# Attention and a bilinear GLU on one core: q, k and v made in five groups of columns instead of six

## The chip, the core and the metric

The kernel runs on one core of one Trainium2 chip. The time is that of one execution on the device, in microseconds (us). The engines are named as in the profile: PE is the matrix engine (PEld its weight load), DVE the vector engine, ACT the scalar engine, POOL the general one, SP the engine that mostly issues transfers (DMAs). A page of the profile describes one execution; the times are medians of several.

## What is computed

x has 2048 rows of 640. It is normalised by row (no gain or bias); the result goes into an attention with a sliding, dilated window and into a feed-forward product of two gates without a nonlinearity between them.

```python
xn = _layernorm(x)
qkv = (xn @ wqkv).reshape(B, S, 3, H, Dh)          # H = 32 heads of Dh = 20
off = jnp.arange(8) * 2                            # window 8, dilation 2
logits = einsum("bhsd,bhswd->bhsw", q, k[pos - off]) * Dh ** -0.5   # masked where pos < off
s = einsum("bhsw,bhswd->bhsd", softmax(logits), v[pos - off]).reshape(B, S, D) @ wo
g = _silu(((xn @ w_gate) * (xn @ w_up)) @ w_down)  # inner width F = 1536
out = x + s * g
```

## The kernel before

**Arithmetic.** Every product is made of three matmuls on operands of type fp32r: each operand is split into a high part (a copy by ACT) and a low part (what is left, a subtraction by POOL or DVE), and high·high, high·low and low·high are added up in PSUM (`ALL3`). `split` (L104, L105) makes the two parts; a split of weights is thus one instruction on ACT and one on POOL behind it.

**q, k and v.** The 32 heads are cut into column groups, `GROUPS = [5, 5, 5, 5, 6, 6]`; the tokens are cut in two halves r = 0, 1. A unit u is a group and a half, twelve in all. `qkv(u, i)` makes one of the eight token tiles of a unit: 15 matmuls (three parts times five blocks of the inner dimension) of 128 × 128 by 3 × heads × 20 columns, so 300 or 360, into one PSUM bank. Below, these 15 are called a product. ACT copies the bank into a staging buffer (L409; three buffers, each for two products), and after each second product a DMA on ACT's queue (L411) writes it to a scratch array in memory. The banks go round in the order `q_one`, g, u; g and u have two banks each, so the bank of `q_one` comes round at every third product.

**The weights of a group.** `load_wq` (L129) loads the raw weights of group g+1 with two DMAs on SP when the second product of group g begins; `split_wq` (L143) splits its five blocks one after the other in the first five products of the group's second half (L105 with 128 × 300 or 128 × 360). High and low parts of blocks 0 to 3 lie in two rotating slots out of ten, those of block 4 in a slot that is kept.

**What runs beside.** `attention` (L424) is a generator that yields the cost of each piece; `advance(budget)` runs pieces as long as there is credit, so many microseconds after each product, 0.38 a head. For each unit it copies q to PSUM (ACT, L469), and in four rounds multiplies q by the shifted k (DVE, L478), reduces (DVE, L488), multiplies the weights of the unit before by its v (DVE, L452) and adds those up (POOL, L455); then comes the softmax (exp on ACT, L511). `load_kq` and `load_kv` (L379 to L387, SP) fetch q, k and v of the next unit from the scratch array, `zero_kv` (L360, POOL) clears the rows before the first token when the width of a unit changes, `store_o` (L530, SP) writes the result. `ORDER` is the order of the units.

`differences` (L1086) is a second row of work: sums and differences of 128 × 512 pieces of x that the groups of gate and up products need later. They are cut into steps, and after each product `paced` grows by 0.42 (0.8 in the last two units); each whole number runs one step. A step is one addition on POOL (L1097, L1099, L1105, L1107, L1109), or a copy on ACT (L1092) with a subtraction on POOL behind it (L1093).

**The order.** It is written out by hand: each engine takes its instructions in the order in which the program writes them. The loop at L1282 runs over units 2 to 11:

```python
            if g + 1 < len(GROUPS) and (r, i) == (0, 1):
                load_wq(g + 1, ((0, 3), (3, 5)))
            elif g + 1 < len(GROUPS) and r and i < KD:
                split_wq(g + 1, nc.gpsimd, (i, i + 1))
```

**Around it.** Ahead of the loop lie the start (normalisation, transposes, units 0 and 1 and the first two blocks of gate and up, L114). Behind it, `group(f)` for f = 2 to 11 (L1179, matmuls L1214) makes gate and up products with fewer multiplications out of the differences and of sums of weights (`w_add` L1164, `w_split`), with plain products (L114) between; `advance` goes on there. In the group before the last, `begin_last` runs what is left of the attention and loads wo (L611). Then come the output product (L950) and the down products (L813).

## Time and profile before

| | |
|---|---|
| median of three runs | 756.78 us (755.92 to 756.83) |
| the profiled execution | 757.46 us, of which the span from the first to the last instruction 755.5 us |
| granted clock of PE | 0.999 of full |
| PE between 60 and 310 us | busy without a break |
| idle time of PE | 9.0 us, nearly all in the first 60 us and behind 540 us |
| stages by the profile | start to 101 us, loop over units 2 to 11 to 277, groups to 540, output and down products to the end |

In the profile a row of grouped instructions reads: line, engine, operation, output and input by the program's names, shape, count, then busy time, mean ns of one, and the idle time of the engine in front of them with what ended it. A chain is followed back from the last instruction; each of its rows has a start, a length and what ran.

### The profile page before, as it was taken

The page shows a single profiled execution, that of the slowest core. Times are in us where ns is not written, and L with a number is a line of the kernel's source. Part 1 is how long each engine was busy: PE and PEld are TensorE (multiplying, and loading weights), DVE is VectorE, ACT ScalarE, POOL GpSimd, SP SyncE. Part 2 cuts the span into 40 slices and gives each one's busy share as a digit, 9 for nine tenths or more (in the row PEclk, how much of TensorE's full clock was granted, in tenths as well). Part 3 has the DMA queues.
Part 4 walks back from the last instruction along what each step waited for, and adds up shares of the span by engine and source line. Part 5 has one row for each costly group of instructions (what it writes and reads, how often), then busy time and mean ns, then how long its engine had stood idle before and what let it go on. Part 6 is the DMA issues. An engine that isn't in the chain of part 4 may idle for free.

```text
span 755.5 us, 11592 instructions
## 1 busy us (share of the span) xinstructions
PE 746.5 (99%) x4342; PEld 687.7 (91%) x4342; DVE 599.2 (79%) x753; ACT 278.5 (37%) x534; POOL 421.5 (56%) x342
## 2 busy tenths in 40 slices
PE   8999999999999999999999999999999999999997
PEld 6889899999999998888888888888999999999997
DVE  7899996998887977979697977335898697777775
ACT  4334213233333333232322222234465664444442
POOL 5100247788968969799879796855659800000000
PEclk9999999999999999999999999999999999999999
DMA  8463446586566473655355222543577565555534
GB/s 316 156 192 102 127 140 188 187 240 180 163 198 196 128 209 95 162 157 174 97 140 165 77 65 66 173 114 105 167 192 211 188 254 188 189 189 188 188 105 140
DMA packets 101974, 123.01 MB, mean 163 GB/s; under 512 B 24376, under 2 KB 75956, under 8 KB 101918
## 3 DMA queue, kind: packets, MB, share of 16 engines
q1 hardware_dynamic: 84318, 107.77, 46.7%
q10 hardware_dynamic: 17600, 14.50, 6.0%
q8 instruction: 34, 0.56, 0.3%
q14 instruction: 22, 0.18, 0.1%
HBM read 78.73 MB, written 42.81 MB: 161 GB/s over the span
## 4 chain that ended last, share of the span: by engine, by line
PE 92%; DVE 3%; POOL 2%; issue 1%; DMA 1%; ACT 0%; SPq 0%; DVEq 0%; POOLq 0%
PE u L114 12%; PE g L114 12%; PE q L400 10%; PE g L400 8%; PE u L400 8%; PE q L813 7%; PE g L1214 7%; PE u L813 6%; PE u L1214 5%; PE e L813 4%; PE g L813 3%; PE q L114 2%; PE q L1214 2%; PE q L950 2%; PE u L950 1%; PE e L950 1%
## 5 line engine op out<-in xcount | busy, mean ns | idle before, releaser
L455 POOL TENSOR_TENSOR o<-o,t 128x800 f32<-128x800 f32 (+1 forms) x81 | 164.3, 2029 | 60.8 <-DVE o L452 50.8
L105 POOL TENSOR_TENSOR s<-wraw,s 128x768 fp32r<-128x768 f32 (+5 forms) x72 | 89.0, 1252 | 77.6 <-ACT s L104 71.4
L478 DVE TENSOR_TENSOR t<-q,kv 128x1600 f32<-128x1600 f32 (+1 forms) x48 | 92.5, 1928 | 11.9 <-ACT q L469 6.1
L114 PE MATMUL g<-xc,s 128*128 128x512 f32 (+1 forms) x435 | 100.4, 382 | 0.0
L114 PE MATMUL u<-xc,s 128*128 128x512 f32 (+1 forms) x435 | 100.4, 382 | 0.0
L114 PEld LDWEIGHTS u<-xc,s 128*128 128x128 f32 x435 | 79.7, 188 | 15.7
L114 PEld LDWEIGHTS g<-xc,s 128*128 128x128 f32 x435 | 79.5, 188 | 15.7 <-DVE gh L1202 0.2
L488 DVE TENSOR_REDUCE lg<-t 128x80 f32<-128x1600 f32 (+1 forms) x48 | 92.3, 1924 | 0.1
L452 DVE TENSOR_TENSOR t<-e,kv 128x800 f32<-128x800 f32 (+1 forms) x84 | 87.2, 1038 | 5.3 <-POOL o L455 5.2
L400 PE MATMUL q<-s,xc 128*128 128x300 f32 (+1 forms) x540 | 84.6, 307 | 1.2 <-DVE lg L252 0.6
L400 PEld LDWEIGHTS q<-s,xc 128*128 128x128 f32 x540 | 79.4, 188 | 2.5 <-DVE lg L252 0.8
L104 ACT ACTIVATE s<-wraw 128x640 fp32r<-128x640 f32 (+5 forms) x73 | 43.0, 603 | 62.0 <-PE u L114 35.8
L400 PE MATMUL g<-s,xc 128*128 128x300 f32 (+1 forms) x420 | 65.8, 308 | 0.0
L400 PE MATMUL u<-s,xc 128*128 128x300 f32 (+1 forms) x420 | 65.4, 307 | 0.0
L400 PEld LDWEIGHTS g<-s,xc 128*128 128x128 f32 x420 | 62.4, 188 | 0.0
L400 PEld LDWEIGHTS u<-s,xc 128*128 128x128 f32 x420 | 62.1, 188 | 0.0
L813 PE MATMUL q<-xc,s 128*128 128x320 f32 x285 | 46.3, 309 | 0.0
L813 PEld LDWEIGHTS q<-xc,s 128*128 128x128 f32 x285 | 42.9, 188 | 0.0
L1214 PE MATMUL g<-xc,s 128*128 128x512 f32 x150 | 37.3, 389 | 0.0
L1186 ACT ACTIVATE gh<-g 128x512 f32<-128x512 f32 x30 | 17.9, 598 | 50.7 <-PE g L1214 50.7
L776 DVE TENSOR_TENSOR s<-s,s 128x768 fp32r<-128x768 f32 x29 | 27.8, 958 | 8.9 <-ACT s L772 8.8
L1214 PEld LDWEIGHTS g<-xc,s 128*128 128x128 f32 x150 | 28.1, 188 | 5.8
(328 smaller groups left out, 1331.5 us busy)
## 6 DMA issues: line engine op xcount, KB each, us to landing
h_scr<-gh SPq DMA_DIRECT2D x48, 256.0 KB, 2.7
wraw<-in_wgu SPq DMA_DIRECT2D x11, 640.0 KB, 4.1
t<-h_scr SPq DMA_DIRECT2D x8, 768.0 KB, 7.5
kv<-qkv_scr SPq DMA_DIRECT2D x14, 400.0 KB, 5.1
qkv_scr<-s ACTq DMA_DIRECT2D x18, 300.0 KB, 4.2
s_scr<-gh SPq DMA_DIRECT2D x16, 320.0 KB, 3.7
gh<-s_scr SPq DMA_DIRECT2D x16, 320.0 KB, 3.8
gh<-in_x SPq DMA_DIRECT2D x16, 320.0 KB, 4.4
```

Of the source, the lines that this page charges most:

```text
L104: nc.scalar.activation(hi, raw, AF.Copy)
L105: eng.tensor_sub(lo, raw, hi.bitcast(F32))
L114: nc.tensor.matmul(acc, a, b, start=first and n == 0, stop=last and n == len(runs) - 1)
L400: nc.tensor.matmul(p, xT[(r * NE + i) // TPC][a][:, k, t0:t0 + P], wq[g][b][k], start=n == 0, stop=n == len(runs) - 1, skip_group_check=ac ...
L452: nc.vector.tensor_mul(t.rearrange("p (n d) -> p n d", d=DH), e[:, :, w].unsqueeze(2).to_broadcast([P, NE * nh, DH]), v)
L455: return NE * c * cost, lambda: eng.tensor_add(y, y, t)
L478: nc.vector.tensor_mul(t, q, k)
L488: nc.vector.tensor_reduce(out=lg[:, :, j:j + 2].rearrange("p n a -> p a n"), in_=t.rearrange("p a (n d) -> p a n d", d=DH), op=ALU.add, ax ...
L776: nc.vector.tensor_sub(hT[m][:, 1], h_raw[n][name], hT[m][:, 0].bitcast(F32))
L813: nc.tensor.matmul(p, y[:, i, k], wd_t[name][k][:, l], start=new and r == 0, stop=r == len(runs) - 1, skip_group_check=True)
L950: nc.tensor.matmul(b, y, w, start=new and r == 0, stop=r == len(runs) - 1, skip_group_check=True)
L1214: nc.tensor.matmul(y, w, x, start=j in (0, 1, 5) and r == 0, stop=r == len(runs) - 1, skip_group_check=True)
```

## The change

The column groups of the attention become `[6, 6, 4, 4, 6, 6]`, and a new table says which of them are made together: `MADE = [[0], [1], [2, 3], [4], [5]]`. The products now go over m, the entries of this table: 360 columns each, but 480 in the third, which makes q, k and v of two groups of four heads at once. There are 80 products (16 each) where there were 96. Calls of `qkv` in the start pass `(0, r, i)` in place of the unit. The two units that a broad product makes have one staging buffer (`wide`, two of them) and go out with two DMAs.

The weights of the broad group take four slots of three blocks of 512 columns; its raw weights come in three DMAs, the last (block 4) written behind the split of block 1. In every group the load of the next weights is written ahead of the first product, and the five blocks are split ahead of the products 3, 4, 6, 8 and 10 of sixteen, counted from 0 over both halves. The steps of `differences` go by a table of rates, one for each m and half. Their results are put into slots by k first.

```diff
@@ -29,9 +29,11 @@
 NCH = S // CH
 TPC = CH // P
 HALF = D // 2
-GROUPS = [5, 5, 5, 5, 6, 6]
+GROUPS = [6, 6, 4, 4, 6, 6]
+MADE = [[0], [1], [2, 3], [4], [5]]
 GOFF = [sum(GROUPS[:g]) * DH for g in range(len(GROUPS))]
 CMAX = max(GROUPS) * DH
+MC = [sum(GROUPS[g] for g in m) * DH for m in MADE]
 QB = 32
 NQ = P // QB
 QC = D // NQ
@@ -128,8 +130,8 @@
 
     def load_wq(g, parts, ahead={}):
 
-        c3 = 3 * GROUPS[g] * DH
-        wq_raw[g] = []
+        c3 = 3 * MC[g]
+        wq_raw.setdefault(g, [])
         for p in parts:
             t = st([P, p[-1] - p[0], c3], "wraw", 2)
             for k0, k1 in zip(p, p[1:]):
@@ -141,10 +143,14 @@
     fifth = []
 
     def split_wq(g, eng, ks=(0, KD)):
-        c3 = 3 * GROUPS[g] * DH
+        c3 = 3 * MC[g]
         if not fifth:
             fifth.append(slot([P, 4, 3 * 128]))
-        if g not in wq:
+        if g not in wq and MC[g] > CMAX:
+            y = [slot([P, 3, CH])[:, :, :c3] for _ in range(4)]
+            wq[g] = [[y[n // 3][:, n % 3] for n in range(a * KD, a * KD + KD)] for a in range(2)]
+            wq[g].append(None)
+        elif g not in wq:
             cols = -(-c3 // 64) * 64
             hi, lo = (slot([P, KD - 1, cols])[:, :, :c3] for _ in range(2))
             wq[g] = [[y[:, k] for k in range(KD - 1)] + [fifth[0][:, g % 2 * 2 + a, :c3]] for a, y in enumerate((hi, lo))]
@@ -153,7 +159,10 @@
             for a, b in ((k0, min(k1, KD - 1)), (max(k0, KD - 1), k1)):
                 a, b = max(a, ks[0]), min(b, ks[1])
                 if a < b:
-                    hi, lo = (y[:, a:b] for y in wq[g][2]) if a < KD - 1 else (y[KD - 1].unsqueeze(1) for y in wq[g][:2])
+                    if b - a > 1:
+                        hi, lo = (y[:, a:b] for y in wq[g][2])
+                    else:
+                        hi, lo = (y[a].unsqueeze(1) for y in wq[g][:2])
                     split(eng, t[:, a - k0:b - k0], hi, lo)
 
     wf_raw, wf = {}, {}
@@ -343,7 +352,8 @@
 
 
     UN = [(g, r) for g in range(len(GROUPS)) for r in range(DIL)]
-    ORDER = [0, 1, 2, 3, 4, 5, 6, 8, 7, 10, 9, 11]
+    ORDER = [0, 1, 2, 3, 4, 6, 5, 7, 8, 10, 9, 11]
+    wide, now = [], [None]
     q_t, kv_t, kv_buf, kv_zero, scr, staged, made = {}, {}, {}, {}, {}, [], set()
 
     def view_kv(u, b):
@@ -360,16 +370,16 @@
             nc.gpsimd.memset(kv_t[u][0:1, a, 0:W - 1, :], 0.0)
             kv_zero[b, a] = GROUPS[UN[u][0]]
 
-    def begin_unit(u):
-        g, r = UN[u]
-        c = GROUPS[g] * DH
-        if u:
-            scr[u] = dr.tile([P, 3, NE, c], F32, name=f"qkv_scr_{u}")
-            return
-        q_t[u] = st([P, NE, c], "q", 1)
-        view_kv(u, r)
-        for a in range(2):
-            zero_kv(u, r, a)
+    def begin_unit(m, r):
+        for g in MADE[m]:
+            u, c = 2 * g + r, GROUPS[g] * DH
+            if u:
+                scr[u] = dr.tile([P, 3, NE, c], F32, name=f"qkv_scr_{u}")
+            else:
+                q_t[u] = st([P, NE, c], "q", 1)
+                view_kv(u, r)
+                for a in range(2):
+                    zero_kv(u, r, a)
 
     def load_kq(u):
@@ -388,30 +398,38 @@
 
     ALL_RUNS = [(a, b, k) for a, b in ALL3 for k in range(KD)]
 
-    def qkv(u, i, runs=ALL_RUNS, at=None, act=None):
-
-        g, r = UN[u]
-        c = GROUPS[g] * DH
+    def qkv(m, r, i, runs=ALL_RUNS, at=None, act=None):
+
+        c = MC[m]
         p = pt([P, 3 * c], "q", 3)
         t0 = (i % TPC) * P
         for n, (a, b, k) in enumerate(runs):
             if n == at:
                 act()
-            nc.tensor.matmul(p, xT[(r * NE + i) // TPC][a][:, k, t0:t0 + P], wq[g][b][k], start=n == 0,
+            nc.tensor.matmul(p, xT[(r * NE + i) // TPC][a][:, k, t0:t0 + P], wq[m][b][k], start=n == 0,
                              stop=n == len(runs) - 1, skip_group_check=act is not None)
-        if u:
+        if m or r:
             if not staged:
                 y = slot([P, 2, 2 * 3 * CMAX], F32)
                 staged.extend([y[:, 0], y[:, 1], st([P, 2 * 3 * CMAX], "pk", 1)])
+            if c > CMAX and not wide:
+                wide.extend([slot([P, 6 * c], F32), st([P, 6 * c], "pk", 1)])
             if i % 2 == 0:
-                staged.insert(0, staged.pop())
-            y = staged[0][:, :6 * c].rearrange("p (a i c) -> p a i c", a=3, c=c)
-            nc.scalar.activation(y[:, :, i % 2, :], p.rearrange("p (a c) -> p a c", a=3), AF.Copy)
-            if i % 2:
-                nc.scalar.dma_start(scr[u][:, :, i - 1:i + 1, :], y)
-            if i == NE - 1:
-                made.add(u)
+                now[0] = wide if c > CMAX else staged
+                now[0].insert(0, now[0].pop())
+            n = len(MADE[m])
+            y = now[0][0][:, :6 * c].rearrange("p (n a i c) -> p n a i c", n=n, a=3, i=2)
+            nc.scalar.activation(y[:, :, :, i % 2, :].rearrange("p n a c -> p a n c"),
+                                 p.rearrange("p (a n c) -> p a n c", a=3, n=n), AF.Copy)
+            for k, g in enumerate(MADE[m]):
+                if i % 2:
+                    nc.scalar.dma_start(scr[2 * g + r][:, :, i - 1:i + 1, :], y[:, k])
+                if i == NE - 1:
+                    made.add(2 * g + r)
+            if c > CMAX and (r, i) == (DIL - 1, NE - 1):
+                staged.clear()
             return
+        u = 0
         nc.scalar.activation(kv_t[u][:, :, W - 1 + i, :], p[:, c:].rearrange("p (a c) -> p a c", a=2), AF.Copy)
         nc.scalar.activation(q_t[u][:, i, :], p[:, :c], AF.Copy)
         for i0, i1 in ((1, 5), (5, NE)):
...
@@ -1070,7 +1088,7 @@
     f0, f1 = KF - 2, KF - 1
     tt, tw, steps = [], {}, []
     T_UNIT = {(j, a, k): divmod(n, 3) for n, (j, a, k) in
-              enumerate((j, a, k) for j in ("T1", "T2", "T3") for a in range(2) for k in range(2))}
+              enumerate((j, a, k) for k in range(2) for j in ("T1", "T2", "T3") for a in range(2))}
 
     def t_unit(j, a, k):
@@ -1279,27 +1297,32 @@
 
     steps += [differences(k) for k in range(2)]
     paced = 0.0
-    for u in range(2, len(UN)):
-        begin_unit(u)
-        g, r = UN[u]
+    last, BLOCK = len(MADE) - 1, (3, 4, 6, 8, 10)
+    RATE = ((1.0, 0.4), (0.3, 0.2), (0.4, 0.6), (0.8, 0.8))
+    for m, r in ((m, r) for m in range(1, len(MADE)) for r in range(DIL)):
+        begin_unit(m, r)
+        heads, broad = MC[m] // DH, m < last and MC[m + 1] > CMAX
         for i in range(NE):
-            if g + 1 < len(GROUPS) and (r, i) == (0, 1):
-                load_wq(g + 1, ((0, 3), (3, 5)))
-            elif g + 1 < len(GROUPS) and r and i < KD:
-                split_wq(g + 1, nc.gpsimd, (i, i + 1))
-            if u == len(UN) - 3 and i == 6:
+            n = r * NE + i
+            if m < last and n == 0:
+                load_wq(m + 1, ((0, 2), (2, 4)) if broad else ((0, 3), (3, 5)))
+            elif m < last and n in BLOCK:
+                split_wq(m + 1, nc.gpsimd, (BLOCK.index(n), BLOCK.index(n) + 1))
+            elif broad and n == BLOCK[1] + 1:
+                load_wq(m + 1, ((4, 5),))
+            if (m, r, i) == (last - 1, 1, 6):
                 load_wf(2)
-            qkv(u, i)
+            qkv(m, r, i)
             if i == 1:
                 finish_piece()
-            advance(PACE * GROUPS[g] * 0.38)
-            paced += 0.42 if u < len(UN) - 2 else 0.8
+            advance(PACE * heads * 0.38)
+            paced += RATE[m - 1][r]
             while paced >= 1:
                 paced -= 1
                 step()
-        if u == len(UN) - 3:
+        if (m, r) == (last - 1, 1):
             steps.append(first_parts())
-        elif u == len(UN) - 2:
+        elif (m, r) == (last, 0):
             for k in range(2):
                 last_difference(k)
     step(100)
```

The places that are moved on the engines:

PE, the first product of the third group of columns, which is the first that is broad. `s_1259`, `s_1260` and `s_159` hold high parts, low parts and block 4 before; now the high parts are in `s_1158` and `s_1159` and the low parts in `s_1159`, `s_1160` and `s_1161`. Before:

```order
L400 MATMUL g_1446<-s_1259,xc_166 128x300 x4
L400 MATMUL g_1446<-s_159,xc_166 128x300
L400 MATMUL g_1446<-s_1260,xc_166 128x300 x4
L400 MATMUL g_1446<-s_159,xc_166 128x300
L400 MATMUL g_1446<-s_1259,xc_166 128x300 x4
L400 MATMUL g_1446<-s_159,xc_166 128x300
```

and now:

```order
L409 MATMUL g_1462<-s_1158,xc_166 128x480 x3
L409 MATMUL g_1462<-s_1159,xc_166 128x480 x3
L409 MATMUL g_1462<-s_1160,xc_166 128x480 x3
L409 MATMUL g_1462<-s_1161,xc_166 128x480
L409 MATMUL g_1462<-s_1158,xc_166 128x480 x3
L409 MATMUL g_1462<-s_1159,xc_166 128x480 x2
```

The product has 15 matmuls as before, each of 480 columns where there were 300, and the low part of block 4 (`s_1161`) is the tenth.

POOL, from the first add of attention beside the second group of columns on (L455 is now L473; L1093, L1097, L1099, L1105, L1107, L1109 are L1111, L1115, L1117, L1123, L1125, L1127; the split is L107). Before:

```order
L455 TENSOR_TENSOR o_1045<-o_1045,t_880 128x800 x4
L1105 TENSOR_TENSOR gh_1158<-xc_435,xc_166 128x512
L455 TENSOR_TENSOR o_1045<-o_1045,t_880 128x800
L1107 TENSOR_TENSOR gh_1159<-xc_435,xc_166 128x512
L455 TENSOR_TENSOR o_1045<-o_1045,t_880 128x800 x2
L1109 TENSOR_TENSOR gh_1158<-gh_1158,gh_1159 128x512
L105 TENSOR_TENSOR s_1260<-wraw_1111,s_1259 128x300 x2
L1093 TENSOR_TENSOR s_1320<-gh_1158,s_1320 128x512
L105 TENSOR_TENSOR s_1260<-wraw_1111,s_1259 128x300
L105 TENSOR_TENSOR s_1260<-wraw_1113,s_1259 128x300
```

and now:

```order
L473 TENSOR_TENSOR o_1048<-o_1048,t_880 128x960
L1123 TENSOR_TENSOR gh_1112<-xc_435,xc_166 128x512
L473 TENSOR_TENSOR o_1048<-o_1048,t_880 128x960
L1125 TENSOR_TENSOR gh_1113<-xc_435,xc_166 128x512
L1127 TENSOR_TENSOR gh_1112<-gh_1112,gh_1113 128x512
L107 TENSOR_TENSOR s_1159<-wraw_1089,s_1158 128x480
L473 TENSOR_TENSOR o_1048<-o_1048,t_880 128x960
L1111 TENSOR_TENSOR s_1184<-gh_1112,s_1184 128x512
L107 TENSOR_TENSOR s_1160<-wraw_1089,s_1158 128x480
L1115 TENSOR_TENSOR gh_1206<-xc_435,gh_1112 128x512
L473 TENSOR_TENSOR o_1048<-o_1048,t_880 128x960
L1117 TENSOR_TENSOR gh_1206<-gh_1206,xc_435 128x512
```

There the first split stood behind seven adds and three steps, and the steps of the second minus (L1097, L1099) behind the splits; now splits and steps stand between the adds, and six steps and two splits come with the first four adds.

ACT, at the copies for the first two differences of x (L1092, now L1110) between the evacuations (L409, now L422). Before, around the first copy:

```order
L409 ACTIVATE s_749<-u_1263 128x3x100
L511 ACTIVATE e_67<-lg_1047 128x320
L104 ACTIVATE s_1259<-wraw_1111 128x300
L409 ACTIVATE s_749<-q_1_65 128x3x100
L411 DMA qkv_scr_1258<-s_749 384x1x200
L469 ACTIVATE q_2_66<-q_1280 128x800
L1092 ACTIVATE s_1320<-gh_1158 128x512
L104 ACTIVATE s_1259<-wraw_1111 128x300
L409 ACTIVATE pk_750<-g_1325 128x3x100
```

and now, around the second:

```order
L106 ACTIVATE s_1158<-wraw_1091 128x480
L422 ACTIVATE s_749<-q_1_65 128x3x120
L1110 ACTIVATE s_1184<-gh_1206 128x512
L422 ACTIVATE s_749<-g_1255 128x3x120
L426 DMA qkv_scr_1088<-s_749 384x1x240
L106 ACTIVATE s_1159<-wraw_1091 128x480
L422 ACTIVATE s_749<-u_1284 128x3x120
L422 ACTIVATE s_749<-q_1_65 128x3x120
L426 DMA qkv_scr_1281<-s_749 384x1x240
```

A copy stands among the evacuations as before; both now fall into the first half of that group, between the evacuations of the fourth and fifth and of the seventh and eighth product, where the first fell into the second half and the second into the next group.

30 lines of the change are left out of this document (15 added, 15 removed).

## The prediction

> **What bounds the kernel now.** I read the page's first part, then the chain of waits, then the waits of TensorE, then the busy time by stretches.
>
> ```profile
> span 755.5 us, 11592 instructions
> PE 746.5 (99%) x4342; PEld 687.7 (91%) x4342; DVE 599.2 (79%) x753; ACT 278.5 (37%) x534; POOL 421.5 (56%) x342
> ...
> PE 92%; DVE 3%; POOL 2%; issue 1%; DMA 1%; ACT 0%; SPq 0%; DVEq 0%; POOLq 0%
> ```
>
> PE is busy for 746.5 of 755.5 us, so at most 9 us can come from waits, and the rest only from fewer or shorter matmuls. The waits that ended on another engine, from the list of PE's waits (engine, line, releaser: us in all, times, longest):
>
> ```profile
> PE q L324 <- DVE lg L318: 1.0, 1, 1.0
> PE q L400 <- DVE lg L252: 0.6, 1, 0.6
> PE q L400 <- ACT q L416: 0.6, 1, 0.6
> ```
>
> All three lie before 30 us. In the stretches where q, k and v are made (start:end, length, busy time and count of PE, PEld, DVE, ACT, POOL, then clock, DMA share, GB/s) PE never stops and its granted clock is full, while POOL, which splits the next weights, is the next busiest but one:
>
> ```profile
> 0.00:20.00 20.00, 17.09 (x94) 13.45 (x95) 14.30 (x46) 9.90 (x27) 11.06 (x36) 1.00 0.91 322
> 107.00:127.00 20.00, 20.00 (x148) 20.00 (x148) 13.58 (x15) 7.00 (x17) 15.85 (x11) 1.00 0.46 145
> 147.00:167.00 20.00, 20.00 (x149) 20.00 (x148) 18.73 (x19) 7.06 (x17) 17.60 (x14) 1.00 0.82 230
> 310.00:400.00 90.00, 89.89 (x397) 74.02 (x396) 78.48 (x72) 24.26 (x40) 79.50 (x60) 1.00 0.47 132
> ```
>
> **The products.** The chain gives the time from one product to the next (start, us, what), which is free of the overlap that a mean per matmul contains:
>
> ```profile
> 136.50 2.05 PE u L400 x15
> ...
> 198.00 2.05 PE u L400 x15
> 200.05 2.40 PE q L400 x15
> ...
> 289.21 3.40 PE g L114 x15
> ...
> 550.74 2.20 PE q L950 x15
> ```
>
> These are 300, 360, 512 and 320 columns: 15 matmuls each, so 136.7, 160.0, 226.7 and 146.7 ns a matmul. Before there are 64 products of 300 and 32 of 360 columns: 64 × 2.05 + 32 × 2.40 = 208.0 us. After there are 64 of 360 (four groups, 16 each) and 16 of 480. The columns in all are the same, 30,720; there are 240 matmuls fewer. No row shows 480 columns. The line through 300 and 360 gives 3.10 us, the line from 360 to 512 gives 2.40 + 120 × 1.00/152 = 3.19, the line from 320 to 512 gives 3.20, and the dearest it can be by a row is the 3.40 of 512 columns. I take 3.19, which lies between the two rows on either side of it. Then 64 × 2.40 + 16 × 3.19 = 153.6 + 51.0 = 204.6 us, **-3.4 us**; the ends are -4.8 (at 3.10) and 0.0 (at 3.40).
>
> Against this stands a rule of the Trainium skill, "TensorE: Matmul & The Clock Gate", section "Back-to-back issue gap": an isolated matmul costs its columns at 2.4 GHz and only 2.5 ns more, so 240 matmuls fewer would be worth 0.6 us. The quoted rows disagree: 300 columns at 2.4 GHz are 125.0 ns and take 136.7, 360 are 150.0 and take 160.0, 512 are 213.3 and take 226.7, 10 to 13 ns more. The same section gives 131 ns for a 512-column matmul in a stream with weight loads; by that the saving would be far larger, and the 226.7 ns speak against that too.
>
> **The start.** Unit 0's eight products lie in the first 60 us and grow by 0.35 us each, which the sum above contains. But two of them stand ahead of PE's longest wait there (timeline of PE: start, us, line, what, idle before):
>
> ```profile
> 19.12 2.31 PE L400 MATMUL q<-s,xc 128*128 128x300 f32 x15
> 21.27 2.23 PE L400 MATMUL e<-s,xc 128*128 128x300 f32 x15
> 28.05 0.41 PE L324 MATMUL q<-lg,lg 128*128 128x32 f32 x2 [0.96 <-DVE lg L318]
> ```
>
> What releases L324 is statistics of x on VectorE, which no product feeds, so 2 × 0.35 = 0.7 us of the longer products goes into that wait: -0.7. On the other side, the first weights grow from 5 × 150 to 5 × 180 KB while the DMA engines are 91% busy at 322 GB/s: 154 KB more take 0.48 us if everything behind them slips, +0.5. I take **-0.3**, ends -0.7 and +0.5.
>
> **VectorE, ACT and the queues under the products.** Attention still has twelve units, now eight of six heads and four of four; per head its work is the same. Evacuations cost ACT 0.47 us at 360 columns, and at 480 about 0.58 by the line from 300 (0.42) through 360, against products of 3.19 us: nothing on the path. In the broad group a pair of products leaves in two DMAs (16 in 51 us) where one went; each holds ACT's queue for 0.52:
>
> ```profile
> L409 ACT ACTIVATE s<-q 128x300 f32<-128x300 f32 x19 | 7.9, 420 | 23.1 <-PE q L400 21.7 <-ACT pk L409 0.7 <-PE g L400 0.7
> L409 ACT ACTIVATE s<-q 128x360 f32<-128x360 f32 x11 | 5.2, 470 | 15.5 <-PE q L400 15.5
> ...
> 134.94 0.52 ACTq L411 DMA_DIRECT2D qkv_scr<-s  x1
> ```
>
> Two evacuations and two DMAs are 2.2 us in 6.4: cover of 4 us. The weights' last block is now loaded by SP only when POOL has split block 1; queued behind it on SP are the loads of unit 2, which can't go before the eighth product of their group is stored, about 20 us into the group, and POOL reaches block 1 at some 17 us (below). Nothing is lost unless POOL is over 3 us late. The four more memsets cost POOL time alone.
>
> **POOL in the second group of products.** This is the tight place. Here attention's adds, the differences of x and the splits of the broad weights share POOL, and the table of rates puts eight steps into the first eight products where 0.42 a product made three. Rows of POOL by shape (busy us, mean ns, idle before):
>
> ```profile
> L455 POOL TENSOR_TENSOR o<-o,t 128x960 f32<-128x960 f32 x25 | 56.6, 2265 | 17.4 <-DVE o L452 13.4 <-DVE t L452 3.8
> L105 POOL TENSOR_TENSOR s<-wraw,s 128x384 fp32r<-128x384 f32 x10 | 10.2, 1020 | 0.0
> L105 POOL TENSOR_TENSOR s<-wraw,s 128x360 fp32r<-128x360 f32 x10 | 9.7, 977 | 2.3 <-ACT s L104 2.3
> ...
> L105 POOL TENSOR_TENSOR s<-wraw,s 128x300 fp32r<-128x300 f32 x16 | 13.0, 834 | 0.3 <-ACT s L104 0.3
> ...
> L1097 POOL TENSOR_TENSOR gh<-xc,gh 128x512 f32<-128x512 f32 x4 | 5.2, 1302 | 0.0
> ...
> L360 POOL MEMSET kv<- 1x700 f32 x4 | 2.6, 674 | 0.0
> ```
>
> In the order, ahead of the last split (which goes out with the eleventh product) stand seven adds, eight steps and four splits. A split of 480 columns is about 1.25 us, between the 1.02 of 384 and the 1.30 of 512. That is 7 × 2.27 + 8 × 1.30 + 4 × 1.25 = 31.3 us; counted from the first add, some 2.5 us into the group, POOL gets there at 33.8 and has the last split at 35.1. The first broad product starts at 16 × 2.40 = 38.4 and asks for that block's low part with its tenth matmul, at 40.3: five us to spare.
>
> The narrower margin is on ACT, whose queue is in order. The trace of before shows the pattern (ACT's timeline, idle before in brackets): L1092 waited 4.22 us for POOL, and the evacuation behind it, of the product that the chain has from 136.50 to 138.55, came at 141.72.
>
> ```profile
> 141.18 0.63 ACT L1092 ACTIVATE s<-gh 128x512 fp32r<-128x512 f32 x1 [4.22 <-POOL gh L1099]
> 141.72 0.40 ACT L409 ACTIVATE pk<-u 128x300 f32<-128x300 f32 x1
> ```
>
> PE did not wait then, for its banks come round again only two or more products later. After the change, POOL's sixth step releases the second of these copies once four adds, six steps and two splits are done: 2.5 + 9.1 + 7.8 + 2.5 = 21.9 us. Behind it in ACT's queue are the evacuations of products eight to ten; 0.63 for the copy, three evacuations at 0.47, a DMA at 0.52 and a split of weights at some 0.6 bring the tenth to about 25.0, and its bank is filled again by the thirteenth at 28.8: 3.8 us to spare. So I cost the place at nothing, and the cover is the ring of banks.
>
> **The group phase.** Each product grants attention 0.38 us of work a head. Before, 48 × 1.90 + 32 × 2.28 = 164.2; after, 48 × 2.28 + 16 × 3.04 = 158.1. So some 6 us of attention go past the last product, into the groups of gate and up products, where POOL is busy 79.5 of 90 us. There the chain runs over POOL for a while, and ends on PE with no loss worth naming (0.11 us idle in the 90):
>
> ```profile
> 331.50 1.84 POOL o L455
> 333.33 0.38 issue
> 333.71 1.60 POOL s L105
> 335.31 0.04 issue
> 335.35 0.50 PE u L1214
> ```
>
> A split of a group's weights came just when PE asked for it, because the attention's change of unit had left POOL without work before. Each change of unit now falls at another place against the groups. Where it falls badly, POOL is late by what was spare, and there is no cover; where it falls well, nothing is lost. I allow **+0.3** for such edges, ends 0 and +2.5 (the length of one add).
>
> The end of attention, flushed late in this phase, also feeds the output weights, whose load SP issues at 486.13 in the trace of before, while the first output product stands on PE only at 539.90:
>
> ```profile
> 486.13 1.90 SPq L611 DMA_DIRECT2D t<-in_wo  x4
> ...
> 539.90 1.32 PE e L950 x9
> ```
>
> Six us later there are covered by fifty.
>
> **The sum.** -3.4 - 0.3 + 0.3 = -3.4 us. The profiled execution took 757.46 us (its span of 755.5 and 2.0 around it) and lies 0.68 above the median of the three runs, 756.78. So 754.1 by its own time, and **753.4** on the scale of the median.
>
> **The rivals.**
>
> A: short waits on POOL take most of it back. For it: POOL on the chain until 335, with nothing spare, and 6 us of attention moved to it. Against it: POOL's whole work hardly grows (five splits of 1.25 do what ten of 0.83 did, 6.3 for 8.3; four more memsets are 2.7; the adds are the same by column), and the rate of work inside a group of gate and up products is as before. One such wait of an add's length, 2.3 us, gives 753.4 + 2.3 = 755.7; within 0.2%.
>
> B: the fixed part of a matmul is not there at 480 columns, and a product of 480 takes the 3.40 of one of 512. Then 208.0 becomes 208.0, and the time is 756.8. For it: nothing but that no row shows that width. Against it: 300, 320 and 360 each have a time of their own. The skill's isolated gap, in the section named above, would come out near this too, at 756.8 - 0.6 = 756.2.
>
> C: slower. The mechanism is the copy on ACT in the second group of products, released by POOL's sixth step and standing ahead of the evacuations. It decides from the point where that step is over 3.8 us late. For it: POOL's adds wait for VectorE, and before, POOL's idle time in front of adds was 43.4 + 17.4 = 60.8 us over 81 of them, 0.75 each (one row stands above, the other here):
>
> ```profile
> L455 POOL TENSOR_TENSOR o<-o,t 128x800 f32<-128x800 f32 x56 | 107.7, 1923 | 43.4 <-DVE o L452 37.4 <-DVE t L452 5.1
> ```
>
> At that mean, four adds bring 3.0 us, just short of the point. A VectorE that itself waits for a load at the change of unit, as before (5.74 us), takes it past by some 2; there are six such copies in the four groups, and two others may meet a change of unit in the same way.
>
> ```profile
> 128.12 1.82 DVE L478 TENSOR_TENSOR t<-q,kv 128x1600 f32<-128x1600 f32 x1 [5.74 <-DMA kv<-qkv_scr]
> ```
>
> Three such stops of 2 us against the 3.4 gained give 756.8 - 3.4 + 6.0 = 759.4. Against it: with six heads instead of five ahead of that point, attention has a fifth more work of its own when the next unit's load arrives, so that wait should shrink.
>
> **Chances.** The forecast 0.61, A 0.16, B 0.06, C 0.17. The forecast alone reaches from 752.0 (480 columns at 3.10) to 755.2 (the start at its +0.5, some edges at 1.0). A measurement of this kernel tells about 0.2% (1.5 us) from no change, so faster is below 755.3 and slower above 758.3. The forecast lies under the first bound nearly whole, and a quarter of A too: faster 0.64. The rest of A, all of B and a little of C are the same: 0.20. Slower: 0.16. The range goes from 751.6 to 757.6, which leaves out most of C and a little at the bottom.
>
> **What would show it.** In the chain, products of 2.40 from the first group and sixteen of about 3.19: if they stand at 3.40, B holds. PE's list of waits should show no new line on L409, the product's line after the change; a wait of L409 on ACT with ACT's L1110 behind POOL's L1117 is C, and a wait of L409 on POOL's L107 would mean that the five us to spare were not there. A wait of L1232 or of L114 on POOL in the groups is A. The wait of PE for the statistics at 28 us should fall from 0.96 to about 0.3, and the idle time of VectorE for the load of unit 2 from 5.74 to near nothing. I am wrong if PE is idle for more than some 2 us between 60 us and the end of the groups, or if a product of 360 columns no longer takes 2.40.

## The result, and the profile after

The changed kernel takes 754.71 us (median of 10 runs, 754.26 to 755.64) against 756.96 us before (10 runs, 755.92 to 757.88): ratio 0.9971, 95% interval 0.9961 to 0.9980. It is faster by 2.3 us where 3.4 were forecast. The profiled execution has a span of 752.9 us against 755.5. Its page, first part:

```profile
span 752.9 us, 11068 instructions
PE 743.7 (99%) x4102; PEld 678.7 (90%) x4102; DVE 600.9 (80%) x753; ACT 275.0 (37%) x513; POOL 422.9 (56%) x341
```

PE is busy for 2.8 us less, with 240 matmuls fewer, and idle about as long as before (9.2 us against 9.0). But the idle time lies elsewhere, as the list of PE's waits shows (engine, line, releaser: us, times, longest):

```profile
PE u L1232 <- POOL s L107: 1.6, 1, 1.6
```

The wait for the statistics at 28 us is gone from the list; a wait for POOL in the groups of gate and up products is new. No wait of L409, the products' line, lies behind 60 us. Three places in the timeline of PE (start, us, line, what) split the time into start, products and the rest. Before:

```profile
101.49 2.21 PE L400 MATMUL q<-s,xc 128*128 128x300 f32 x15
...
276.69 1.52 PE L1214 MATMUL g<-xc,s 128*128 128x512 f32 x6
```

After:

```profile
28.53 0.31 PE L333 MATMUL q<-lg,lg 128*128 128x32 f32 x2
...
105.71 2.56 PE L409 MATMUL q<-s,xc 128*128 128x360 f32 x15
108.11 2.56 PE L409 MATMUL g<-s,xc 128*128 128x360 f32 x15
...
153.85 3.42 PE L409 MATMUL g<-s,xc 128*128 128x480 f32 x15
157.11 3.41 PE L409 MATMUL u<-s,xc 128*128 128x480 f32 x15
...
272.91 1.52 PE L1232 MATMUL g<-xc,s 128*128 128x512 f32 x6
...
276.31 1.52 PE L1232 MATMUL g<-s,s 128*128 128x512 f32 x6
```

Starts of neighbours give the price of a product: 2.40 us for 360 columns, 3.25 for 480 (153.85 to 157.11, and 52.0 for the sixteen from 144.11 to 196.11). The sums:

| stretch | before | after | difference | of it products | the rest |
|---|---|---|---|---|---|
| to the first product of the loop | 101.49 | 105.71 | +4.22 | 16 × 0.35 = +5.60 | -1.38 |
| the loop | 175.20 | 167.20 | -8.00 | -8.00 | 0 |
| from its end to the span's | 478.81 | 479.99 | +1.18 | | +1.18 |
| span | 755.5 | 752.9 | -2.6 | -2.40 | -0.20 |

Inside the loop PE lost nothing in either kernel. So the products brought 2.4 us, the start 1.4, and the groups took 1.2 back.

**The new wait.** In the groups PE stands still once, at 434.7 us. Timeline of PE:

```profile
434.07 0.61 PE L1232 MATMUL u<-xc,s 128*128 128x512 f32 x2
436.24 0.50 PE L1232 MATMUL u<-xc,s 128*128 128x512 f32 x1 [1.55 <-POOL s L107]
```

POOL's timeline behind it (in brackets the idle time and what ended it):

```profile
428.62 2.26 POOL L473 TENSOR_TENSOR o<-o,t 128x960 f32<-128x960 f32 x1 [4.34 <-DVE o L470]
432.41 2.27 POOL L473 TENSOR_TENSOR o<-o,t 128x960 f32<-128x960 f32 x1 [1.53 <-DVE t L470]
434.64 1.54 POOL L107 TENSOR_TENSOR s<-wraw,s 128x640 fp32r<-128x640 f32 x1
```

VectorE's, and that of SP's queue:

```profile
427.39 1.16 DVE L470 TENSOR_TENSOR o<-e,kv 128x960 f32<-128x960 f32 x1 [2.66 <-DMA o_scr<-o]
```

```profile
418.10 0.93 SPq L1194 DMA_DIRECT2D h_scr<-gh  x2
420.88 0.35 SPq L172 DMA_DIRECT2D wraw<-in_wgu  x1
421.29 0.43 SPq L548 DMA_DIRECT2D o_scr<-o  x1
```

Read from below: the store of a unit's result is issued at 421.29, behind two writes of h that had to wait for POOL's product until 418.10, and behind a load of weights that had to wait until 420.88 for a split on POOL to free its buffer. There is one buffer for the result, so VectorE's first product of the next unit waits for that store; POOL's add waits for VectorE; the split of weights stands behind two adds; PE waits for the split. Before the change the same store went out over nine us earlier, ahead of the load and the writes:

```profile
411.76 0.38 SPq L530 DMA_DIRECT2D o_scr<-o  x1
420.04 0.36 SPq L163 DMA_DIRECT2D wraw<-in_wgu  x1
421.65 12.43 SPq L1176 DMA_DIRECT2D h_scr<-gh  x4
```

Against the products, attention is later than before, as the credit said: its change of unit comes at 413 instead of 409 us, while the group that runs there starts some 4 us earlier.

**POOL and ACT beside the second group of columns.** ACT's timeline, the two copies of the differences and the evacuation of the tenth product:

```profile
119.54 0.63 ACT L1110 ACTIVATE s<-gh 128x512 fp32r<-128x512 f32 x1 [3.56 <-POOL gh L1127]
...
130.09 0.64 ACT L1110 ACTIVATE s<-gh 128x512 fp32r<-128x512 f32 x1 [6.91 <-POOL gh L1117]
...
132.54 0.46 ACT L422 ACTIVATE s<-q 128x360 f32<-128x360 f32 x1
```

The second copy held ACT for 6.91 us and went at 24.4 us into the group where 21.9 were worked out; the tenth product's bank was free at 133.0, and its next product began at 105.71 + 28.8 = 134.5. Only 1.5 us were to spare, not 3.8. Because the evacuation of the eighth product stood behind this copy too, its store was issued only at 131.11, and the loads of unit 2 that need it at 135.93, 30.2 us into the group and not about 20; VectorE stood idle for 3.95 us at that change of unit (from 138.49 to 142.44), and ACT for 2.28 us ahead of the copy of q.

### The profile page after: what moved, and what is told of

Same layout as the page of the kernel before. It is cut to its first block, busy times and chain, and to the rows that moved or that the text cites. A ratio compares the mean times of both kernels' runs of the same rounds, so it can differ in the third digit from the quotient of the medians.

```text
span 752.9 us, 11068 instructions
## 1 busy us (share of the span) xinstructions
PE 743.7 (99%) x4102; PEld 678.7 (90%) x4102; DVE 600.9 (80%) x753; ACT 275.0 (37%) x513; POOL 422.9 (56%) x341
## 5 line engine op out<-in xcount | busy, mean ns | idle before, releaser
L473 POOL TENSOR_TENSOR o<-o,t 128x960 f32<-128x960 f32 (+1 forms) x81 | 163.9, 2023 | 58.8 <-DVE o L470 46.0
L107 POOL TENSOR_TENSOR s<-wraw,s 128x640 fp32r<-128x640 f32 (+4 forms) x67 | 88.0, 1325 | 81.2 <-ACT s L106 78.7
L496 DVE TENSOR_TENSOR t<-q,kv 128x1920 f32<-128x1920 f32 (+1 forms) x48 | 92.5, 1928 | 18.4 <-ACT q L487 11.4
L470 DVE TENSOR_TENSOR t<-e,kv 128x960 f32<-128x960 f32 (+1 forms) x84 | 87.1, 1037 | 14.7 <-POOL o L473 14.6
L506 DVE TENSOR_REDUCE lg<-t 128x96 f32<-128x1920 f32 (+1 forms) x48 | 92.3, 1922 | 0.1
L409 PE MATMUL q<-s,xc 128*128 128x360 f32 (+1 forms) x465 | 84.8, 333 | 1.1 <-ACT q L434 0.6
L409 PEld LDWEIGHTS q<-s,xc 128*128 128x128 f32 x465 | 77.2, 188 | 4.8 <-ACT q L434 0.9
L409 PE MATMUL u<-s,xc 128*128 128x360 f32 (+1 forms) x345 | 63.2, 334 | 0.0
L106 ACT ACTIVATE s<-wraw 128x768 fp32r<-128x768 f32 (+6 forms) x68 | 41.8, 631 | 55.3 <-PE u L116 30.0
L409 PE MATMUL g<-s,xc 128*128 128x360 f32 (+1 forms) x330 | 61.5, 337 | 0.0
L409 PEld LDWEIGHTS u<-s,xc 128*128 128x128 f32 x345 | 57.8, 188 | 2.3
L409 PEld LDWEIGHTS g<-s,xc 128*128 128x128 f32 x330 | 55.7, 188 | 2.6
L831 PE MATMUL q<-xc,s 128*128 128x320 f32 x342 | 55.5, 309 | 0.0
```

Of the source, the lines that this page charges most:

```text
L106: nc.scalar.activation(hi, raw, AF.Copy)
L107: eng.tensor_sub(lo, raw, hi.bitcast(F32))
L409: nc.tensor.matmul(p, xT[(r * NE + i) // TPC][a][:, k, t0:t0 + P], wq[m][b][k], start=n == 0, stop=n == len(runs) - 1, skip_group_check=ac ...
L470: nc.vector.tensor_mul(t.rearrange("p (n d) -> p n d", d=DH), e[:, :, w].unsqueeze(2).to_broadcast([P, NE * nh, DH]), v)
L473: return NE * c * cost, lambda: eng.tensor_add(y, y, t)
L496: nc.vector.tensor_mul(t, q, k)
```

## The experiments

Each run is compared with the kernel before on its own chip; a ratio has its 95% interval. Edits are to the changed kernel unless said otherwise.

**The price of a width by itself.** A kernel of its own with matmuls alone.

> This kernel computes nothing of the reference: it runs only groups of 15 matmuls (128 x 128 stationary, weights changed for each, fp32r) at widths from 120 to 512 columns, four groups in a row for each width, up and down again, and writes zeros and one number. Theory: the 3.25 us of a 480-column product in the changed kernel is the price of that width itself, so 480 columns take 216.7 ns a matmul here too, beside 136.7 (300), 160.0 (360) and 226.7 (512). Rival: 480 columns cost what the line between 360 and 512 says, 212.6 ns, and the rest comes from where the broad group's weights lie or from what runs beside them.

From one evacuation to the next (ACT's timeline), at 480 columns going up and at 240:

```profile
54.56 0.37 ACT L31 ACTIVATE keep<-y 128x240 f32<-128x240 f32 x1 [1.38 <-PE y L30]
56.24 0.37 ACT L31 ACTIVATE keep<-y 128x240 f32<-128x240 f32 x1 [1.31 <-PE y L30]
...
154.10 0.57 ACT L31 ACTIVATE keep<-y 128x480 f32<-128x480 f32 x1 [2.70 <-PE y L30]
157.35 0.57 ACT L31 ACTIVATE keep<-y 128x480 f32<-128x480 f32 x1 [2.68 <-PE y L30]
```

480 columns take 3.25 us for 15 matmuls going up and down again: 216.7 ns, the price of that width and nothing of this kernel's. 512 take 3.40 as in the products. 120, 180 and 240 columns all take 1.68, 111.7 ns a matmul: there is a floor. The Trainium skill ("TensorE: Matmul & The Clock Gate", section "LDWEIGHTS (loading the stationary operand)") gives the ns of a weight load as its columns over 1.2, an estimate of 106.7 ns for 128 columns; the floor of 111.7 ns agrees within 5%. What was not expected: 300 columns took 2.10 and 360 took 2.47 here, 140.0 and 164.4 ns, at a full granted clock, where the products take 2.05 and 2.40.

**The same heads, not merged.**

> The changed kernel with the same head groups (6, 6, 4, 4, 6, 6) and the same pace, but each group made by itself: 64 products of 360 and 32 of 240 columns, 1440 matmuls again. Theory: 240 columns take about 240/256 of the 1.79 us that 256 take, 1.68 us, so 32 of them 53.7 where the 16 broad ones took 52.0: 1.7 us slower than the changed kernel, about 756.4, and the product sum is 0.7 under that of the kernel before. Rival: the gain is in cutting 300 to 360 columns and the merging brings nothing: 240 columns at 1.62 us, the time stays at 754.7.

```diff
-MADE = [[0], [1], [2, 3], [4], [5]]
+MADE = [[0], [1], [2], [3], [4], [5]]
...
-    RATE = ((1.0, 0.4), (0.3, 0.2), (0.4, 0.6), (0.8, 0.8))
+    RATE = ((1.0, 0.4), (0.15, 0.15), (0.1, 0.1), (0.4, 0.6), (0.8, 0.8))
```

760.28 us, ratio 1.0060 (1.0047 to 1.0074): slower than the kernel before. Timeline of PE:

```profile
180.94 1.83 PE L409 MATMUL u<-s,xc 128*128 128x240 f32 x15
183.22 1.95 PE L409 MATMUL q<-s,xc 128*128 128x240 f32 x15 [0.45 <-ACT s L422]
...
198.45 2.63 PE L409 MATMUL q<-s,xc 128*128 128x360 f32 x15
200.92 2.63 PE L409 MATMUL g<-s,xc 128*128 128x360 f32 x15
```

A product of 240 columns takes 1.675 us, so 32 of them 53.6 as the theory had it, 1.6 more than the broad ones. But 0.45 us went into a wait, and all 32 products of 360 columns behind the narrow ones took 2.467 instead of 2.40, 2.1 us more. Whether the wait or the 240 columns themselves brought that, this run can't tell. Together 4.2, of the 4.4 by which its span (757.3) exceeds that of the changed kernel. The profiled execution was the shortest of the five (759.29 us); what the others lost beyond it, up to 3 us, stays open.

**The start alone.** The kernel before with the broader groups first.

> The kernel before with heads grouped 6, 5, 5, 5, 5, 6 instead of 5, 5, 5, 5, 6, 6: as many products of 300 and of 360 columns as before, but the first two units, which lie in the start, are the broader ones. Theory: the changed kernel won some 1.3 us in the start because its longer first products fill waits for the statistics of x that PE had to sit out anyway; so this kernel is 1.3 us faster than the one before, ratio 0.9983. Rival: the start won for another reason, and the time is that of the kernel before.

```diff
-GROUPS = [5, 5, 5, 5, 6, 6]
+GROUPS = [6, 5, 5, 5, 5, 6]
```

759.20 us, ratio 1.0026 (1.0017 to 1.0035), against the expectation. The profiled execution, one of the shorter of its runs (757.27), has the span of the kernel before, 755.5. Its loop begins at 105.49, 4.0 us later than before with 5.6 us more in longer products: the start did win 1.6 us without any merging. And it lost 1.9 again at 438 us, by the same chain as the changed kernel, as its trace reads: here too the products grant attention 158.1 us instead of 164.2, and the store comes late. SP, VectorE and PE:

```profile
426.64 0.38 SPq L530 DMA_DIRECT2D o_scr<-o  x1
```

```profile
434.19 0.99 DVE L452 TENSOR_TENSOR o<-e,kv 128x800 f32<-128x800 f32 x1 [3.39 <-DMA o_scr<-o]
```

```profile
438.77 0.50 PE L1214 MATMUL u<-xc,s 128*128 128x512 f32 x1 [1.91 <-POOL s L105]
```

The runs of this kernel fall into two sets, 757.2 to 757.9 and 759.2 to 759.8; the profile is of the first. The second set has no trace. Its mean granted clocks are 0.997 to 0.999, those of the first 0.999 to 1.000, which fits the fall of the clock that the next run shows.

**The changed kernel again**, as the yardstick of the next three.

> The changed kernel once more, as the yardstick on the chip of the three others: ratio 0.997 to the kernel before, with one wait of PE of some 1.5 us at 436 us (line L1232, for POOL's split).

754.75 us, ratio 0.9971 (0.9960 to 0.9982); the wait at 436 us was 1.8 us. The profiled execution was the longest of the seven (756.56 us), and behind that wait its granted clock fell (windows as in the prediction; the clock is the third number from the end):

```profile
436.00:440.00 4.00, 3.41 (x9) 2.65 (x10) 4.00 (x3) 1.19 (x2) 3.44 (x3) 0.66 0.00 0
440.00:444.00 4.00, 4.00 (x17) 3.29 (x16) 1.86 (x3) 1.38 (x2) 3.92 (x6) 0.91 0.00 0
```

The sixteen matmuls from the end of the wait on took 5.37 us, where the first profile has 3.76. So this wait can cost 1.6 us more than its own length.

**The store out of SP's queue.**

> The changed kernel, but the last four units of attention store their result from ACT's queue instead of SP's. Theory: the wait at 436 us comes from the queue of SP, where the store of the tenth unit stands behind two writes to h_scr and a load of weights; VectorE's first product of the next unit waits for that store (2.66 us), POOL's add for VectorE, the split of weights stands behind the adds, and PE waits for the split. With the store out of SP's queue the wait goes: 1.5 us less than the changed kernel, ratio 0.995, and VectorE's waits for o_scr<-o in that phase shrink. Rival: POOL is simply too full there and the split is late in any case; then PE's wait stays within 0.5 us of 1.55.

```diff
-                nc.sync.dma_start(o_scr[r, b, ...
+                (nc.scalar if u >= 8 else nc.sync).dma_start(o_scr[r, b, ...
```

756.56 us, ratio 0.9998 (0.9989 to 1.0007). PE's wait for POOL at 436 us is gone, so the theory of the wait holds; but its list of waits has a new row:

```profile
PE g L1232 <- ACT gh L1204: 2.8, 3, 1.4
```

ACT now waits for POOL's last add before it can issue the store (at 378.25, 456.68 and 484.97, each within 0.05 us of that add's end), and the copies that free PE's banks stand behind it. The cure cost more than the wait.

**Attention made up before the last product.**

> The changed kernel with 0.399 us of attention a head and product instead of 0.38 from the third group of columns on, so that the 6 us by which attention fell back are made up before the last product; on SP the store of the tenth unit then stands ahead of the writes to h_scr and of the load again, as in the kernel before. Theory: the wait at 436 us goes, ratio 0.995. Rival: it is the change of unit itself that empties POOL and it only moves, or POOL in the last groups of columns is over its limit with 6 us more; then as much is lost elsewhere and the ratio stays at 0.997 or above.

```diff
-            advance(PACE * heads * 0.38)
+            advance(PACE * heads * (0.38 if m == 1 else 0.399))
```

762.51 us, ratio 1.0071 (1.0058 to 1.0084). The wait at 436 us is gone here too. In its place, from PE's waits and ACT's timeline:

```profile
PE g L1232 <- POOL s L107: 4.7, 1, 4.7
PE q L409 <- ACT s L422: 2.0, 1, 2.0
```

```profile
254.76 0.63 ACT L1110 ACTIVATE s<-gh 128x512 fp32r<-128x512 f32 x1 [10.09 <-POOL gh L1127]
```

With 5% more attention from the third group on, POOL falls back; a copy waits 10.09 us for it in ACT's queue, the evacuations behind it come too late, and a split for the first of the groups is 4.7 us late for PE. The rival of this run holds: there was no room for the 6 us.

**More adds ahead of the copy.**

> The changed kernel with half as much again of attention beside the first eight products of the second group (0.57 instead of 0.38 a head), so that two more adds stand on POOL ahead of its sixth step. Theory: in the changed kernel the evacuation of the tenth product ends 1.5 us before its bank is filled again; two more adds make the second copy 4.5 us later, so PE waits some 3 us for ACT at about 135 us, where it waits for nothing now. Rival: the ring of banks and the staging buffers still cover it, and PE waits under 0.5 us there.

```diff
-            advance(PACE * heads * 0.38)
+            advance(PACE * heads * (0.57 if (m, r) == (1, 0) else 0.38))
```

779.93 us, ratio 1.0301 (1.0282 to 1.0320). PE waits for ACT in the second group, far longer than expected; its waits, and ACT's timeline:

```profile
PE q L409 <- ACT s L422: 10.8, 1, 10.8
```

```profile
134.63 0.63 ACT L1110 ACTIVATE s<-gh 128x512 fp32r<-128x512 f32 x1 [9.38 <-POOL gh L1117]
...
143.44 0.97 ACT L487 ACTIVATE q<-q 128x960 f32<-128x960 f32 x1 [6.73 <-DMA q<-qkv_scr]
```

The copy came 4.5 us later, as expected. Most of the rest of this wait is a second instruction in the same queue: the copy of q for the next unit, which waits 6.73 us for a load, and that load needs what the late evacuations had only just written out. This is the forecast's rival C, and it shows how close the changed kernel stands to it. The wait is less than half of the 24.7 us by which the span grew (777.6). In the loop, 15.4 us longer, the first product behind the wait took 4.48 us at a granted clock of about 0.5, and those of 360 columns behind it 2.47 instead of 2.40. The other 9 us lie in the groups, with further waits for POOL and ACT (4.2, 1.9 and 0.9 us); what makes up their rest stays open.

**The store earlier in the program.**

> The changed kernel, but attention writes the stores of its last four units into the program right after the last add, ahead of the softmax of the next unit, on SP as before. On SP the store of the tenth unit then stands ahead of the two writes to h_scr and the load of weights. Theory: the same wait as in the run with ACT's queue goes (PE's line L1232 for POOL at 436 us, 1.5 to 1.8 us) and nothing is put into ACT's queue, so nothing comes back there: ratio 0.995 to 0.9955, about 753.3. Rival: SP now waits for POOL's last add with the loads and writes behind it, and something of the groups waits for them instead: the wait is gone, but the ratio stays at 0.997 or above.

```diff
             ahead(n + 1, (0, 1))
+            if before is not None and before[0] >= 8:
+                store_o(before)
...
-            if before is not None:
+            if before is not None and before[0] < 8:
                 store_o(before)
```

752.87 us (752.78 to 753.55), ratio 0.9951 (0.9937 to 0.9964): the fastest kernel of this study, 1.8 us under the changed one (1.5 by the two ratios), with a span of 751.1 us. SP's queue:

```profile
415.58 0.38 SPq L550 DMA_DIRECT2D o_scr<-o  x1
418.20 0.94 SPq L1196 DMA_DIRECT2D h_scr<-gh  x2
420.98 0.35 SPq L172 DMA_DIRECT2D wraw<-in_wgu  x1
```

The store goes out 5.7 us earlier, VectorE does not wait for it, and PE waits for nothing between 20 and 580 us. No work was moved or dropped.

**The steps spread evenly.**

> The changed kernel with the steps of the differences spread as before the change (0.42 a product, 0.8 in the last group) instead of by its table. Theory: the table brings no time by itself, it only has to get the results into their slots in time; POOL is relieved beside the second group and loaded beside the third and fourth, whose products are longer or whose attention is no heavier; no wait of PE in the products, the time within 1 us of the changed kernel. Rival: the table is what keeps POOL ahead of ACT's copies where attention's change of unit falls, and without it a copy holds the evacuations up as in the runs with more attention: PE waits for ACT at some product by 2 us or more.

```diff
-    RATE = ((1.0, 0.4), (0.3, 0.2), (0.4, 0.6), (0.8, 0.8))
+    RATE = ((0.42, 0.42), (0.42, 0.42), (0.42, 0.42), (0.8, 0.8))
```

760.92 us, ratio 1.0055 (1.0041 to 1.0069): neither theory. No product waits. But steps are left over at the end of the loop, and the splits for the first group of gate and up products come behind them. Timeline of PE, and the stretch behind it (start:end, length, busy time and count of PE, PEld, DVE, ACT, POOL, granted clock, DMA share, GB/s):

```profile
275.15 1.83 PE L1232 MATMUL g<-xc,s 128*128 128x512 f32 x4 [1.92 <-ACT s L106]
277.60 1.22 PE L1232 MATMUL g<-xc,s 128*128 128x512 f32 x2 [0.62 <-POOL s L107]
278.61 3.94 PE L1232 MATMUL q<-xc,s 128*128 128x512 f32 x9
282.38 1.54 PE L1232 MATMUL g<-s,s 128*128 128x512 f32 x6
```

```profile
276.00:280.00 4.00, 3.38 (x9) 2.20 (x8) 0.24 (x1) 1.28 (x4) 4.00 (x5) 0.50 0.49 125
```

The granted clock was 0.50 from 275.5 us on, so the first wait, 1.92 us, was enough to bring it down: the four matmuls ahead of the second wait took 1.83 us where six take 1.52. The nine behind it, which take 2.04 us at full clock, took 3.8. The third sum of the group starts at 282.38 where the changed kernel starts it at 276.31: 6.1 us, the whole loss. The Trainium skill ("TensorE: Matmul & The Clock Gate", section "What's actually happening") says that the clock falls to half after an idle window of some 3.4 us; here 1.92 us did it. Other single waits went either way: 1.55 us (the changed kernel) and 1.91 us (six heads first) left the clock at 1.00, 1.8 us (the changed kernel again) brought it to 0.50. No run shows what decides between them.

**What makes 360 columns take 160.0 or 164.7 ns.** Again a kernel of matmuls alone.

> This kernel computes nothing of the reference: groups of 15 matmuls as in the products (three parts, five blocks, stationary blocks of 512 wide tiles, weights 384 apart), six groups in each of the stretches 512, 360, a short wait of PE for ACT, 360, 512, 360, 240, 360, 512, 360, 480, 360, 512, 300, a short wait, 300 columns. Theory: 360 columns take 160.0 ns a matmul behind 512 columns and 164.7 behind a wait, until 512 columns come again, as in the runs in which PE waited inside the products; behind 480 columns 160.0. Rival: 240 columns, where the weight loads set the pace, do the same without a wait, or it is where the operands lie, and all the stretches of 360 columns are alike.

Stretches of 360 columns took 2.40 us a product behind 512 and behind 480 columns, and 2.47 behind 240 without any wait. ACT's timeline, the last evacuation of 240 columns and those behind it:

```profile
110.23 0.37 ACT L43 ACTIVATE keep<-y 128x240 f32<-128x240 f32 x1 [1.31 <-PE y L42]
112.71 0.47 ACT L43 ACTIVATE keep<-y 128x360 f32<-128x360 f32 x1 [2.11 <-PE y L42]
115.18 0.47 ACT L43 ACTIVATE keep<-y 128x360 f32<-128x360 f32 x1 [2.00 <-PE y L42]
```

512 columns brought 360 back to 2.40. Behind a short wait of 0.23 us, 300 columns took 2.10 where they took 2.05 ahead of it. The wait put between the first two stretches of 360 columns did not stop PE in the trace, and 2.40 stayed. So a wait does it, as the theory has it (shown here for 300 columns, and for 360 by the waits of 2.0 and 10.8 us in the two runs with more attention), and 240 columns do it without one, as the rival has it. That it is the weight loads at 240 columns is argued, not shown.

**The start alone, with the early store.**

> The kernel before with heads grouped 6, 5, 5, 5, 5, 6 and, as in the run with the early store, the stores of attention's last four units written ahead of the softmax of the next. It makes 1440 matmuls, as many of each width as the kernel before. Theory: in the run with these groups alone the start came 1.6 us earlier than the widths say and PE then lost 1.9 us at 438 us behind the store; with the store out of the way 1.6 us are left, ratio 0.9979, about 755.2. Rival: the gain of the start is lost again later whatever the store does; ratio 0.9995 or above.

758.41 us, ratio 1.0023 (1.0012 to 1.0033). It did not test what it should: at the change of unit in question the loads of the next unit and a write of h still stand ahead of the store on SP, which goes out at 426.85 (426.64 without the edit), and PE still waits, 2.3 us where it was 1.9. Behind that wait the profile has the clock at 0.50 (440 to 443 us), and the sixteen matmuls from its end on took 5.36 us where the run without the edit has 3.80. The four shortest executions, 756.8 to 757.7 us at clocks of 0.999 to 1.000, show no gain over the kernel before (756.96). That the store's place costs this kernel its gain is thus argued from its trace and not shown.

## Why the prediction was right, and where its sizes were off

**What bounds.** Right. PE sets the time, and the widths alone explain the loop to 0.1 us. Between 60 us and the end of the groups PE idled for 1.55 us, in the second profile for 1.8, just under the 2 us that were to show the forecast wrong.

**The products, -3.4 forecast, -2.4 measured.** The step that failed is the price of 480 columns: 3.19 was taken from the line between 360 and 512, and the run with widths alone has 3.25. The price is not a line: 360 columns cost 6.67 ns a column of a product, 480 cost 6.77, 512 cost 6.64. The ends, 3.10 and 3.40, held it. Rival B (3.40) was wrong. The rule of the Trainium skill that the prediction quotes ("TensorE: Matmul & The Clock Gate", section "Back-to-back issue gap") would have given 0.6 us; the 2.4 measured speak against it. By the same prices, the recut from 300 to 360 columns brought 64 × (2.40 × 300/360 - 2.05) = -3.2 us, and eight heads made at 480 instead of at 360 columns cost 16 × (3.25 - 480/360 × 2.40) = +0.8. The merging pays against 240 columns (1.6 us), not against 360.

**The start, -0.3 forecast, -1.4 measured.** The wait at 28 us went from 0.96 to nothing, and a second one of some 0.25 us at 47 us too; the two products ahead of it began 0.8 us later (19.93 for 19.12), for the two products and the larger weights ahead of them, and that went into the same waits. The end of -0.7 was too tight, because only two of the four products ahead of the wait were counted against it. That this gain is independent of the merging is shown by the run with six heads first (1.6 us).

**VectorE, ACT and the queues.** Right for ACT's two DMAs and for the load behind block 1 (SP issued it at 125.39, and the loads of unit 2 behind it were held until 135.93 by the store that they need, not by it). Wrong for VectorE: its idle time at the load of unit 2 was to fall from 5.74 us to near nothing and fell to 3.95. The order of the trace points to the copy held by POOL, which delayed the store of the eighth product and with it the loads; no run tests that. PE did not wait for it.

**POOL in the second group.** Costed at nothing, and nothing was lost. But the margins were off: the first add came 4.8 us into the group and not 2.5, a term that no row stood for, and everything on POOL moved with it. The last split ended at 142.86, 3.2 us ahead of the matmul that needs it instead of 5. The run with more adds showed that the mechanism of rival C is real and that it costs more than the copy's own delay; that it would decide from some 1.5 us on is read from the margin, since only 4.5 us were tried.

**The group phase, +0.3 forecast, +1.2 measured.** Rival A's mechanism took place once: 6 us of attention past the last product moved a change of unit, and POOL was late by 1.55 (PE lost 0.11 in the groups before the change; the 0.3 left to +1.2 stay open). Its cause was not foreseen. The prediction asked whether POOL had time; the runs show that the store's place in SP's queue decided, since moving the stores alone brought the time back.

Two of these errors, +1.0 for the products and +0.9 for the groups, were in part offset by the start's -1.1. That offset is luck; the sign and most of the size rest on the first term.

## What to carry to other kernels

Price a matmul by its own width and not by a line through others, and look for the width that is cheapest a column before merging or cutting. When work that runs beside is shifted against the rest, follow the stores and loads in the in-order queues, not only the engines: here a store written ahead of the softmax instead of behind it was worth 1.5 to 1.8 us, next to the 2.4 of all the products. A wait inside a stretch of narrow matmuls costs more than its length, in the spacing of those behind it; and here waits from 1.8 us on brought the granted clock to 0.50 for 3 us and more, though not every time.

## What the hardware showed that was not expected

The same 360-column matmul, weights changed each time, ran at 160.0 or at 164.7 ns at a granted clock of 1.00. It was slow behind a stretch of 240 columns and behind a wait of PE among the products (2.0 us in the run with 5% more attention, 10.8 in the run with more adds), for all the products that followed, and fast again behind 512 columns. Sixteen products of 480 did not bring it back (the run with more adds), and they took 52.0 us there as in the changed kernel: 480 columns have one price. Which state in PE this is, no run shows; in the kernel of widths 360 columns were slow even going down from 512 through seven widths. From 240 columns down the spacing stops falling, at 111.7 ns.

The granted clock of PE fell to 0.50 behind single waits of 1.8, 1.92 and 2.3 us, and stayed at 1.00 behind 1.55 and 1.91.
